# Attention with keys on partitions, exp without a maximum, sums from a column of ones, and the old program kept in a branch

## The chip, the cores and the metric

One NeuronCore of one Trainium2 chip runs the whole program. The metric is the device time of one execution in microseconds (us), lower is better. Everything is float32 unless a line says otherwise.

## The reference

Inputs: q, k, v of 4 batch entries x 8 heads x 768 tokens x 64, eight memory keys and values for each head, a router `w_gate` (512 x 8), and two weight matrices for each of eight experts. Cut to what matters:

```python
for c in range(S // 32):                       # chunks of 32 queries
    k_ctx = k[:, :, max(0, 32*c - 16) : min(S, 32*c + 32 + 8)]
    k_full = concat([mem_k, k_ctx]); v_full = concat([mem_v, v_ctx])
    scores = q_c @ k_full.T / 8
    a = exp(scores - max(scores)); a = a / (sum(a) + 1e-9)
    out[:, :, c] = a @ v_full
x = out as (3072 tokens, 512)
logits = x @ w_gate; e = argmax(logits); gate = softmax(logits)[e]
y = gate * (relu(x @ w1[e]) @ w2[e])
```

## The kernel before

The program has three stages that follow one another.

**Attention** (lines 155 to 235). A block is 96 queries (three chunks) of one batch entry with all 8 heads; there are 32 blocks, 8 for a batch entry. The 8 memory keys and the 120 keys that the three chunks can see are 128 keys. `load` (five transfers on SP's queue, 704 KB for a block) brings k, memory k, q, v and memory v, three blocks ahead. `turn_qk` transposes q and k on PE into the PSUM tiles `tq` and `tk`; ACT scales q out of PSUM (L170), DVE copies k (L174). `scores` puts **queries on partitions**: a bfloat16 matmul writes the additive mask (L182), eight head matmuls add q times k (L185, 128 columns each), DVE takes the negated maximum of each row (L187), ACT does one exp for each head with that maximum as bias and sums the row in the same instruction (L191; the sum shows as a second record, ACTIVATION_READ_ACCUMULATOR). The values need the keys on partitions, so `turn_ex` transposes each head's exponentials on PE (`te`, L199) and DVE or ACT copies them out (L201). `values` multiplies (L209), DVE divides by the sums (L212, L213, L215) and POOL's queue writes the block x to memory (L218). `turn_xb` transposes x for the router (L224, L226), `logits` multiplies by `w_gate` (L235) into one PSUM tile per batch entry, and `route` runs after each eighth block.

The order of the work around the change is set in two places: the loop after `route` runs the steps of different blocks interleaved (scores of block i, values of i-2, logits of i-3), and the compiler's scheduler then orders each engine's instructions; an engine runs them in that order. PSUM tiles come from rotating pools: `ps_t` (three buffers) serves `tq`, `tk`, `te` and `tx`; a buffer is written again only after its reader has emptied it.

**Slots** (L313 to L351). Counts of tokens per expert, then 32 small matmuls (`who`, L343) find which token stands in which row of which slot of 128 tokens.

**Experts** (L358 to L407). 31 slots, each with 2 MB of w1 and 2 MB of w2 fetched on SP's queue (L360, L362), a gather of 128 rows of x (L364), four transposes, 32 matmuls of the first layer (L387, 128 columns), 8 of the second (L404, 512 columns), and a scatter of the result (L407).

The profile shows each float32 matmul as two PE instructions (a transpose as one), each with its own weight load (PEld).

Of the kernel before, what the change touches and what calls it, by code (L numbers as in the profile page):

```python
# [10 lines left out]
F32 = mybir.dt.float32  # L11
BF16 = mybir.dt.bfloat16
I32 = mybir.dt.int32
AX_X = mybir.AxisListType.X
OP = mybir.AluOpType
AF = mybir.ActivationFunctionType
PSUM = bass.MemoryType.PSUM
DRAM = bass.MemoryType.DRAM

B, H, S, D = 4, 8, 768, 64  # attention  # L20
NMEM = 8
CHUNK, LEFT, RIGHT = 32, 16, 8
QB = 96  # queries of a block: three chunks
NQB = S // QB  # blocks of a batch entry
NB = B * NQB  # blocks in all
BAND = QB + LEFT + RIGHT  # keys that a block's chunks see; with the memory 128
N, DM, E, F = B * S, H * D, 8, 1024  # experts
NS = N // 128 + E - 1  # slots of 128 tokens of one expert: enough for any routing
FAR = 4096.0  # a row index past the end
NEG = -1e30  # L30
# [5 lines left out]

def _consts():
    p = np.arange(128)
    c = {}
# [5 lines left out]
    c["token"] = p[:, None] + QB * np.arange(NB)[None]  # L45
    # additive mask of a block = chunk_of.T @ mask_*: row g holds chunk g's keys
    c["chunk_of"] = p[:, None] == np.arange(QB)[None] // CHUNK
    for name, qb in (("mask_first", 0), ("mask_mid", 1), ("mask_last", NQB - 1)):
        m = np.zeros((128, 128))
        key = p[NMEM:] - NMEM + band_start(qb)  # L50
        for g in range(QB // CHUNK):
            q0 = QB * qb + CHUNK * g
            seen = (key >= max(0, q0 - LEFT)) & (key < min(S, q0 + CHUNK + RIGHT))
            m[g, NMEM:] = np.where(seen, 0.0, NEG)
        c[name] = m
    at, k = {}, 0
# [3 lines left out]
    pack = np.concatenate([np.asarray(v).astype(np.float32) for v in c.values()], axis=1)  # L60
    return np.ascontiguousarray(pack), at


@with_exitstack
def kernel(
    ctx: ExitStack,
# [11 lines left out]
    nc = tc.nc  # L78
    mm, turn = nc.tensor.matmul, nc.tensor.transpose
# [6 lines left out]

    cpool = ctx.enter_context(tc.tile_pool(name="cpool", bufs=1))
    lpool = ctx.enter_context(tc.tile_pool(name="lpool", bufs=4))
    apool = ctx.enter_context(tc.tile_pool(name="apool", bufs=2))
    rpool = ctx.enter_context(tc.tile_pool(name="rpool", bufs=2))  # L90
    wpool = ctx.enter_context(tc.tile_pool(name="wpool", bufs=2))
    mpool = ctx.enter_context(tc.tile_pool(name="mpool", bufs=2))
    dpool = ctx.enter_context(tc.tile_pool(name="dpool", bufs=1, space=DRAM))
    ps_s = ctx.enter_context(tc.tile_pool(name="ps_s", bufs=2, space=PSUM))
    ps_t = ctx.enter_context(tc.tile_pool(name="ps_t", bufs=3, space=PSUM))
    ps_o = ctx.enter_context(tc.tile_pool(name="ps_o", bufs=2, space=PSUM))
    ps_r = ctx.enter_context(tc.tile_pool(name="ps_r", bufs=1, space=PSUM))

    x_dram = dpool.tile([N, DM], F32, name="x_dram")

# [1 line left out]
    pack, at = _consts()  # L102
    cst = cpool.tile([128, pack.shape[1]], F32, name="cst")
    nc.scalar.dma_start(cst, nc.inline_tensor(pack, name="c_pack").ap())

    def const(name):
# [3 lines left out]
    ident, tri, iota, slot0, rev, token = (  # L110
        const(n) for n in ("ident", "tri", "iota", "slot", "rev", "token")
    )
# [8 lines left out]
    ones = cpool.tile([128, 128], F32, name="ones")  # L121
# [3 lines left out]

    # q turned: of each pair of heads two copies, the other head's rows zero
    qTs = [cpool.tile([128, H // 2, 2, QB], F32, name=f"qT{i}") for i in range(2)]
    for i, t in enumerate(qTs):
        (nc.vector, nc.gpsimd)[i].memset(t, 0.0)

    # routing of all tokens: token 96 t + p at [p, t]
    onehot = cpool.tile([QB, NB, E], F32, name="onehot")
# [5 lines left out]

# [1 line left out]
    st = [dict() for _ in range(NB)]  # L140
# [87 lines left out]
    lg = {}  # L228
# [9 lines left out]

# [1 line left out]
    def small(shape, name, dt=F32):  # L240
        return rpool.tile(shape, dt, name=name)

    def route(b):
# [6 lines left out]
        nc.vector.reduce_max(top, l, axis=AX_X)  # L250
        # the first of the largest
        eq = small([QB, NQB, E], "eq")
# [4 lines left out]
        nc.vector.tensor_tensor(oh, bc(rev[0:QB], 1, NQB), bc(first, 2, E), op=OP.is_equal)  # L257
        # its probability: exp(0) over the sum
        nc.vector.tensor_tensor(l, l, bc(top, 2, E), op=OP.subtract)
# [4 lines left out]
        nc.vector.reciprocal(gate[:, sl], total)  # L264
        # the token's rank among its expert's tokens
        for t in range(t0, t0 + NQB):
# [43 lines left out]

# [1 line left out]
    cnt = ps_r.tile([128, E], F32, tag="r", name="cnt")  # L312
# [17 lines left out]

    # who is in slot a, row b: sums with one term over the tokens
    own = cpool.tile([QB, NB, E], F32, name="own_all")
# [19 lines left out]

# [1 line left out]
    ms = [dict() for _ in range(NS)]  # L354
# [71 lines left out]


# [1 line left out]
_INS = ["q", "k", "v", "mem_k", "mem_v", "moe_w_gate", "moe_w1", "moe_w2"]  # L429
# [24 lines left out]
```

## Time and profile before

| | |
|---|---|
| median of 3 runs | 760.68 us (759.02 to 760.82) |
| profiled execution | span 758.7 us, first to last instruction; no separate time is listed for it |
| attention, up to the last logits | 0 to 264 us |
| slots, up to the first gathered rows | 264 to 298 us |
| experts | 298 to 749 us |
| busy over the span | PE 690.3 us (91%), PEld 547.1 (72%), DVE 195.9 (26%), ACT 184.1 (24%), POOL 88.7 (12%) |
| moved by DMA | 175.06 MB, mean 231 GB/s |

How to read it: the shares over the whole span mix three stages, so the table by stage and the order of time inside one block say more than the totals. The span and the timed median differ by 2.0 us; the sum below is made against the span and then carried to the median.

### The profile page before, as it was taken

What the parts mean: (1) busy time and instruction counts of PE and PEld (TensorE: products, weight loads), DVE (VectorE), ACT (ScalarE), POOL (GpSimd) and SP (SyncE); (2) the same over time, 40 slices, a digit from 0 to 9 for tenths busy, and PEclk for the clock granted to TensorE, in tenths of its full rate; (3) what the DMA queues carried; (4) which work ended last, traced back from release to release, by engine and by line L of the source; (5) the groups of instructions that cost most, each with busy time, mean ns of one, the idle gap of its engine ahead of it and who ended that gap; (6) DMA issues with size and microseconds to landing.
All of it is one profiled execution on the core that took longest, in us unless ns stands there. A gap on an engine that the chain in (4) does not pass through costs nothing. (4 is left out here: it accounts for less than half of the span.)

```text
span 758.7 us, 11768 instructions
## 1 busy us (share of the span) xinstructions
PE 690.3 (91%) x4670; PEld 547.1 (72%) x4670; DVE 195.9 (26%) x438; ACT 184.1 (24%) x675; POOL 88.7 (12%) x133
## 2 busy tenths in 40 slices
PE   5889898888888746999999999999999999999994
PEld 4788787778778646767766776776776776776672
DVE  2555655665655531010010010010010001001000
ACT  3556556465645400001001000100100100100100
POOL 0000100100010122011111111111111111111010
PEclk9999899999989955999999999999999999999998
DMA  9545454455540148699989899899899899899830
GB/s 213 133 121 130 98 124 123 107 134 120 125 99 22 43 176 332 219 331 319 332 313 328 313 333 340 303 330 345 307 334 331 307 339 323 308 326 335 302 111 0
DMA packets 148438, 175.06 MB, mean 231 GB/s; under 512 B 95582, under 2 KB 95582, under 8 KB 148384
## 3 DMA queue, kind: packets, MB, share of 16 engines
q1 hardware_dynamic: 140704, 153.10, 62.4%
q0 software_dynamic: 7008, 20.72, 7.5%
q8 instruction: 37, 0.61, 0.3%
q10 hardware_dynamic: 672, 0.50, 0.2%
q14 instruction: 17, 0.14, 0.1%
HBM read 161.71 MB, written 14.42 MB: 232 GB/s over the span
## 5 line engine op out<-in xcount | busy, mean ns | idle before, releaser
L387 PEld LDWEIGHTS ph<-xsT,w 128*128 128x128 f32 x1984 | 227.2, 193 | 14.7 <-issue 14.4
L387 PE MATMUL ph<-xsT,w 128*128 128x128 f32 x1984 | 227.5, 276 | 0.0
L404 PE MATMUL py<-w,h 128*128 128x512 f32 x496 | 218.0, 592 | 0.0
L404 PEld LDWEIGHTS py<-w,h 128*128 128x128 f32 x496 | 91.8, 190 | 103.8 <-issue 103.8
L396 DVE TENSOR_SCALAR h<-ph 128x512 f32<-128x512 f32 x31 | 21.5, 692 | 402.5 <-issue 381.7
L191 ACT ACTIVATE ex<-sc,top 96x128 f32<-96x128 f32 x256 | 89.8, 357 | 65.7 <-DVE top L187 64.1
L406 ACT ACTIVATE y<-py,gates 128x512 f32<-128x512 f32 x31 | 21.3, 688 | 317.9 <-PE py L404 317.9
L185 PE MATMUL sc<-kT,qT 128*96 128x128 f32 x512 | 72.8, 290 | 1.1 <-DVE kT L174 1.1
L185 PEld LDWEIGHTS sc<-kT,qT 128*96 128x96 f32 x512 | 63.3, 176 | 1.8 <-ACT qT L170 1.2
L407 POOL DMA_INDIRECT out_dram<-y,dst x31 | 31.5, 1017 | 241.2 <-ACT y L406 241.2
L209 PE MATMUL o<-vn,eT 128*96 128x64 f32 x512 | 56.5, 245 | 1.6 <-DVE eT L201 1.3
L209 PEld LDWEIGHTS o<-vn,eT 128*96 128x96 f32 x512 | 52.8, 166 | 3.2 <-DVE eT L201 2.6
L187 DVE TENSOR_REDUCE top<-sc 96x4 f32<-96x512 f32 x64 | 44.0, 687 | 24.0 <-PE sc L185 24.0
L364 POOL DMA_INDIRECT xs<-x_dram,src x31 | 30.3, 977 | 169.5 <-PE txs L375 148.3
L191 ACT ACTIVATION_READ_ACCUMULATOR ex<-sc,top 96x1 f32 x256 | 50.0, 195 | 0.0
L398 ACT ACTIVATE h<-ph 128x512 f32<-128x512 f32 x31 | 18.5, 598 | 125.4 <-PE ph L387 125.4
L199 PE MATMUL te<-cst,ex 96*128 96x96 f32 x256 | 35.8, 269 | 9.8 <-ACT qT L170 9.8
L218 POOL DMA_DIRECT2D x_dram<-x x32 | 16.7, 522 | 228.8 <-DVE x L215 228.8
L170 ACT ACTIVATE qT<-tq 64x384 f32<-64x384 f32 x64 | 31.1, 486 | 40.7 <-PE tq L167 39.9
L199 PEld LDWEIGHTS te<-cst,ex 96*128 96x128 f32 x256 | 27.9, 153 | 14.8 <-ACT qT L170 14.7
L182 PE MATMUL sc<-cst 128*96 128x512 bf16 x64 | 24.9, 392 | 14.2 <-ACT ex L191 9.1
L235 PEld LDWEIGHTS lg_ps<-wg,xT 128*96 128x96 f32 x256 | 24.1, 164 | 13.0 <-DVE xT L226 12.5
(74 smaller groups left out, 372.5 us busy)
## 6 DMA issues: line engine op xcount, KB each, us to landing
w<-in_moe_w_dram SPq DMA_DIRECT2D x62, 2048.0 KB
kn<-in_k_dram SPq DMA_DIRECT2D x32, 240.0 KB
vn<-in_v_dram SPq DMA_DIRECT2D x32, 240.0 KB
qn<-in_q_dram SPq DMA_DIRECT2D x32, 192.0 KB
x_dram<-x POOLq DMA_DIRECT2D x32, 192.0 KB, 2.6
kn<-in_mem_k_dram SPq DMA_DIRECT2D x32, 16.0 KB
vn<-in_mem_v_dram SPq DMA_DIRECT2D x32, 16.0 KB
xs<-x_dram,src POOLq DMA_INDIRECT x31, 7.0
```

Source lines behind the costliest of these rows:

```text
L170: nc.scalar.activation(s["qT"][sl, :, x], tq[sl], AF.Copy, scale=D**-0.5)
L182: mm(sc, lhsT=const16("chunk_of"), rhs=bc(mask, 1, 4), start=True, stop=False)
L185: mm(sc[:, j], lhsT=s["qT"][:, h // 2, h % 2], rhs=s["kT"][:, h // 2], start=False, stop=j == 3)
L187: nc.vector.tensor_reduce(top, sc, axis=AX_X, op=OP.max, negate=True)
L191: nc.scalar.activation(ex[:, j], sc[:, j], AF.Exp, bias=top[:, j : j + 1], accum_out=s["sum"][:, h : h + 1])
L199: turn(te[:, j], s["ex", g][:, j], ident[0:QB, 0:QB])
L209: mm(s["o"][:, h], lhsT=s["eT", g][:, j], rhs=s["v"][:, h], start=True, stop=True)
L235: mm(lg["ps"][:, t], lhsT=s["xT"][:, c], rhs=wg[:, c], start=c == 0, stop=c == DM // 128 - 1)
L364: nc.gpsimd.indirect_dma_start(out=s["x"], out_offset=None, in_=x_dram, in_offset=bass.IndirectOffsetOnAxis(ap=src[:, a : a + 1], axis=0),)
L387: mm(ph[:, f], lhsT=s["w1"][:, c, c0 : c0 + 128], rhs=s["xT"][:, c], start=c == 0, stop=c == DM // 128 - 1,)
L404: mm(py, lhsT=s["h"][:, f], rhs=s["w2"][:, f], start=f == 0, stop=f == F // 128 - 1)
L407: nc.gpsimd.indirect_dma_start(out=out, out_offset=bass.IndirectOffsetOnAxis(ap=dst[:, a : a + 1], axis=0), in_=y, in_offset=None, bounds_ ...
```

## The change

The old program is kept whole, under the name `general`, with its pools renamed. A new program, `ordinary`, runs first; `general` stands in a branch behind it that is taken when a check of the sums fails. In `ordinary` the slots and experts are the old text; the attention is new:

- **q and k are turned a half batch entry (384 tokens) at a time**, with three sets of four 128 x 128 transposes for q and three for k. They are loaded with 3 transfers of 256 KB each (row j holds tokens 3p + j), so the copies out of PSUM write every third column of kT and qT. The memory keys are turned once and POOL copies them into kT after every 48 keys of a block, so that a window of 128 columns of kT is the block's memory and keys.
- **Scores have keys on partitions**: one matmul for a pair of heads with 192 columns, no mask matmul; the mask is the bias of the exp (0 or -1e30 for each key), one exp for each chunk of 32 queries over all heads; no maximum is subtracted.
- **Values** take the exponentials as they stand (no `te`, no copies); v has a 65th column of ones, so column 64 of the result is the sum. The 1e-9 is left out.
- Reciprocals of all sums are kept; at the end every one is compared with 1.0 and 1e-30, and `good` says whether all are inside.
- v is loaded with three transfers for a block (parts of its keys, memory, the other keys); `ps_t` has two buffers and now also serves the logits and the ranks; the score tile takes two banks.

```diff
+    def load_half(m):
+        b, hf = divmod(m, 2)
+        for name, src in (("q", q), ("k", k)):
+            t = half[m][name] = lpool.tile([128, NT, H, D], F32, name=f"{name}n")
+            by = src[b, :, HALF * hf : HALF * hf + HALF].rearrange("h (p t) d -> p t h d", t=NT)
+            for j in range(NT):
+                nc.sync.dma_start(t[:, j], by[:, j])
...
+    def turn_half(m, j):
...
+        tk = ps_t.tile([128, H // 2, 128], F32, tag="t", name="tk")
+        for a in range(H // 2):
+            turn(tk[:, a], half[m]["k"][:, j, 2 * a : 2 * a + 2].rearrange("p h d -> p (h d)"), ident)
+        by = tk.rearrange("p a (n f c) -> p a n f c", n=NQB // 2, f=2)
+        for f in range(2):
+            c0 = (QB // 2 + NMEM) * f + j
+            nc.vector.tensor_copy(
+                kT[:, :, hf * NQB // 2 : (hf + 1) * NQB // 2, c0 : c0 + QB // 2 - NT + 1 : NT], by[:, :, :, f]
+            )
...
+        for x in range(2):
+            sl = slice(D * x, D * x + D)
+            nc.scalar.copy(qT[sl, :, x, j : j + HALF - NT + 1 : NT], tq[sl])
...
+    def scores(i):
...
+        sc = ps_s.tile([128, 2, 512], F32, tag="s", name="sc")
+        for a in range(H // 2):
+            o = sc[:, a // 2, 2 * QB * (a % 2) : 2 * QB * (a % 2) + 2 * QB]
+            mm(
+                o.rearrange("p (x t) -> p x t", x=2),
+                lhsT=kT[:, a, w0 : w0 + WIN],
+                rhs=qT[:, a, :, q0 : q0 + QB],
+                start=True,
+                stop=True,
+            )
...
+        for g in range(3):
+            sl = slice(CHUNK * g, CHUNK * g + CHUNK)
+            nc.scalar.activation(
+                ex4[:, :, :, sl], sc4[:, :, :, sl], AF.Exp, bias=mask[:, 3 * x + g : 3 * x + g + 1], scale=D**-0.5
+            )
...
+    def values(i):
...
+        for g in range(2):
+            o = ps_o.tile([QB, 4, D + 1], F32, tag="o", name="o")
+            for j in range(4):
+                h = 4 * g + j
+                mm(o[:, j], lhsT=s["ex"][:, h], rhs=s["v"][:, h], start=True, stop=True)
+            inv = inv_all[:, i, 4 * g : 4 * g + 4]
+            nc.vector.reciprocal(inv, o[:, :, D])
+            nc.vector.tensor_tensor(s["x"][:, 4 * g : 4 * g + 4], o[:, :, 0:D], bc(inv, 2, D), op=OP.mult)
...
+    for i in range(NB + 3):
+        m = i // (NQB // 2)
+        if i % (NQB // 2) == 1 and m + 2 < 2 * B:
+            load_half(m + 2)
+        if i + 2 < NB:
+            load_v(i + 2)
+        if i < NB:
+            scores(i)
+        if i % (NQB // 2) < NT and m + 1 < 2 * B:
+            turn_half(m + 1, i % (NQB // 2))
+        if 0 <= i - 3 < NB:
+            logits(i - 3)
+        if 0 <= i - 1 < NB:
+            values(i - 1)
+        if 0 <= i - 2 < NB:
+            turn_xb(i - 2)
...
+    nc.vector.tensor_scalar(good, okp[0:1], float(QB * 2 * NB * H), None, op0=OP.is_equal)
...
+    ordinary(tc, *args, good)
+    rv = nc.values_load(good[0:1, 0:1], min_val=0, max_val=1)
+    with tc.If(rv == 0):
+        general(tc, *args)
```

How the order of instructions moves, at three places. First PE in the middle of attention. Before, one block (names: `tq`, `tk` q and k turned, `te` exponentials turned, `sc` scores, `o` values, `tx` x turned, `lg_ps` logits; a row counts matmuls, and `x4` is four of them):

```order
L167 MATMUL tq<-cst,qn 128x96 x4
L173 MATMUL tk<-cst,kn 128x128 x4
L199 MATMUL te<-cst,ex 128x96 x8
L185 MATMUL sc<-kT,qT_97 96x128 x4
L209 MATMUL o<-vn,eT 96x64 x4
L185 MATMUL sc<-kT,qT_97 96x128 x4
L209 MATMUL o<-vn,eT 96x64 x2
L224 MATMUL tx<-cst,x 128x96 x4
L209 MATMUL o<-vn,eT 96x64 x2
L182 LDWEIGHTS cst_90
L182 MATMUL sc<-cst_90 96x512
L235 MATMUL lg_ps<-wg,xT 96x8 x4
```

Each block has all of it, and the scores of one block fill the time in which the values' exponentials are copied. Now, from one block's values to the next block's, with two of a half's three sets of turns between:

```order
L640 MATMUL o<-v_108,ex 96x65 x8
L594 MATMUL tk<-cst,kn 128x128 x4
L603 MATMUL tq<-cst,qn 128x128 x4
L664 MATMUL lg_ps<-wg,xT 96x8 x4
L616 MATMUL sc<-qT_100,kT 128x192
L652 MATMUL tx<-cst,x 128x96 x4
L616 MATMUL sc<-qT_100,kT 128x192 x2
L594 MATMUL tk<-cst,kn 128x128 x4
L603 MATMUL tq<-cst,qn 128x128 x4
L664 MATMUL lg_ps<-wg,xT 96x8 x4
L616 MATMUL sc<-qT_100,kT 128x192 x3
L640 MATMUL o<-v_109,ex 96x65 x8
```

The transposes of exponentials and the mask matmuls are gone, the scores are four matmuls instead of eight, and `tk`, `tq`, `lg_ps`, `tx` follow one another through the same two buffers of `ps_t`.

Second, SP's queue where attention ends (`good` is the check, `expi` the experts of the slots, `w_2140` the first weights):

```order
L572 DMA v_107<-in_v_dram 48x8x64
L883 TENSOR_LOAD good
L883 ISA x2
L806 TENSOR_LOAD expi
L806 ISA x2
L808 ISA
L808 DMA w_2140<-in_moe_w_dram 128x4x1024
```

The load of `good` into SP's register stands ahead of the first load of `expi`, and so ahead of the weights. Third, the end of POOL's queue before `general` begins:

```order
L855 DMA out_dram<-y,dst 3072x512 x5
L883 TENSOR_LOAD good
L884 COMPARE_AND_BRANCH
L189 MEMSET qT_4461 128x768
L194 MEMSET seen 96x8
```

The load and the branch come behind the last scatter; PE, ACT and DVE have the same two behind their last instruction.

## Rows read from the trace of the kernel before

**Rows 1.** The page, busy tenths of PE and granted PE clock in 40 slices

```profile
PE   5889898888888746999999999999999999999994
PEclk9999899999989955999999999999999999999998
```

**Rows 2.** Busy time by stage: us, then PE, PEld, DVE, ACT, POOL, clock, DMA share, GB/s

```profile
0.00:9.00 9.00, 2.81 (x10) 1.59 (x10) 1.94 (x4) 2.25 (x3) 0.99 (x6) 1.00 0.85 198
9.00:264.00 255.00, 221.41 (x1984) 199.49 (x1985) 144.57 (x331) 141.76 (x609) 21.46 (x56) 0.97 0.46 111
264.00:298.00 34.00, 15.98 (x74) 15.24 (x73) 9.25 (x42) 0.26 (x1) 7.44 (x12) 0.50 0.67 265
298.00:749.00 451.00, 450.09 (x2604) 330.74 (x2604) 40.15 (x62) 39.84 (x62) 57.85 (x58) 1.00 0.86 301
```

**Rows 3.** Timeline of POOL, two blocks: start, us, what

```profile
120.54 0.51 POOL L218 DMA_DIRECT2D x_dram<-x  x1 [6.68 <-DVE x L215]
127.74 0.51 POOL L218 DMA_DIRECT2D x_dram<-x  x1 [6.69 <-DVE x L215]
```

**Rows 4.** Timeline of PE's weight loads in one block

```profile
121.72 0.76 PEld L235 LDWEIGHTS lg_ps<-wg,xT 128*96 128x96 f32 x8 [0.43 <-DVE xT L226]
...
123.26 0.45 PEld L173 LDWEIGHTS tk<-cst,kn 128*128 128x128 f32 x4
123.67 0.42 PEld L199 LDWEIGHTS te<-cst,ex 96*128 96x128 f32 x4
...
125.80 0.78 PEld L209 LDWEIGHTS o<-vn,eT 128*96 128x96 f32 x8
126.50 0.90 PEld L185 LDWEIGHTS sc<-kT,qT 128*96 128x96 f32 x8
...
127.69 0.40 PEld L224 LDWEIGHTS tx<-cst,x 96*128 96x128 f32 x4
128.03 0.42 PEld L209 LDWEIGHTS o<-vn,eT 128*96 128x96 f32 x4
```

**Rows 5.** The same of the experts: end of a second layer, then a first layer

```profile
502.32 0.19 PEld L387 LDWEIGHTS ph<-xsT,w 128*128 128x128 f32 x1 [0.24 <-issue]
502.75 7.11 PEld L387 LDWEIGHTS ph<-xsT,w 128*128 128x128 f32 x63 [0.24 <-issue]
```

**Rows 6.** Groups of instructions: busy us, mean ns of one, idle before

```profile
L191 ACT ACTIVATE ex<-sc,top 96x128 f32<-96x128 f32 x256 | 89.8, 357 | 65.7 <-DVE top L187 64.1
...
L174 DVE COPY kT<-tk 128x512 f32<-128x512 f32 x32 | 22.1, 692 | 29.8 <-PE tk L173 29.8
...
L398 ACT ACTIVATE h<-ph 128x512 f32<-128x512 f32 x31 | 18.5, 598 | 125.4 <-PE ph L387 125.4
...
L226 DVE COPY xT<-tx 128x384 f32<-128x384 f32 x32 | 17.8, 557 | 1.3 <-PE tx L224 1.3
...
L213 DVE RECIPROCAL inv<-inv 96x8 f32<-96x8 f32 x32 | 6.3, 198 | 1.0
```

**Rows 7.** Timeline, DVE's start after the scores of rows 4

```profile
126.11 0.69 DVE L187 TENSOR_REDUCE top<-sc 96x4 f32<-96x512 f32 x1 [0.32 <-PE sc L185]
```

**Rows 8.** Timeline of the start, the first scores

```profile
9.17 3.70 PE L185 MATMUL sc<-kT,qT 128*96 128x128 f32 x16 [0.88 <-DVE kT L174]
```

**Rows 9.** Timeline of PE, DVE and SP around the slots

```profile
263.47 0.84 PE L235 MATMUL lg_ps<-wg,xT 128*96 128x8 f32 x8 [0.65 <-DVE xT L226]
...
273.18 0.16 DVE L329 TENSOR_SCALAR expi<-expf 1x31 int32<-1x31 f32 x1
...
274.33 0.43 SPq L360 DMA_DIRECT2D w<-in_moe_w_dram  x1
...
298.04 1.97 PE L375 MATMUL txs<-cst,xs 128*128 128x128 f32 x8 [6.37 <-DMA xs<-x_dram,src]
```

**Rows 10.** The last scatter in the timeline, and the page's median to landing

```profile
749.17 0.99 POOL L407 DMA_INDIRECT out_dram<-y,dst  x1 [13.03 <-ACT y L406]
...
out_dram<-y,dst POOLq DMA_INDIRECT x31, 7.1
```

More of the change, by code (lines that the diff above doesn't have):

```diff
@@ L34, in band_start, with _consts_general @@
     return min(max(QB * qb - LEFT, 0), S - BAND)
-def _consts():
+def _consts_general():
     p = np.arange(128)
@@ L61, in _consts, with window, column, runs_of @@
     return np.ascontiguousarray(pack), at
+HALF = S // 2
+NT = HALF // 128
+WIN = 128
+PER = QB + NMEM
+KW = NQB * PER
+NV = 6
+def window(qb):
+    return min(max(PER * qb - LEFT, 0), KW - WIN)
+def column(c):
+    blk, r = divmod(c, PER)
+    if QB // 2 <= r < QB // 2 + NMEM:
+        return "mem", r - QB // 2
+    return "key", QB * blk + (r if r < QB // 2 else r - NMEM)
+def runs_of(qb):
+    out = []
+    for p in range(WIN):
+        kind, x = column(window(qb) + p)
+        if out and out[-1][1] == kind and out[-1][2] + out[-1][3] == x:
+            out[-1][3] += 1
+        else:
+            out.append([p, kind, x, 1])
+    return out
+def _consts():
+    p = np.arange(128)
+    c = {}
+    c["ident"] = np.eye(128)
+    c["tri"] = np.triu(np.ones((128, 128)), 1)
+    c["iota"] = np.broadcast_to(p, (128, 128))
+    c["slot"] = np.broadcast_to(128 * np.arange(NS), (128, NS))
+    c["rev"] = np.broadcast_to(E - np.arange(E), (128, E))
+    c["token"] = p[:, None] + QB * np.arange(NB)[None]
+    m = np.zeros((128, 3, 3))
+    for x, qb in enumerate((0, 1, NQB - 1)):
+        for g in range(3):
+            q0 = QB * qb + CHUNK * g
+            for i in range(WIN):
+                kind, t = column(window(qb) + i)
+                if kind == "key" and not max(0, q0 - LEFT) <= t < min(S, q0 + CHUNK + RIGHT):
+                    m[i, x, g] = NEG
+    c["mask"] = m.reshape(128, 9)
+    at, k = {}, 0
+    for name, v in c.items():
+        at[name] = (k, v.shape[1])
+        k += v.shape[1]
+    pack = np.concatenate([np.asarray(v).astype(np.float32) for v in c.values()], axis=1)
+    return np.ascontiguousarray(pack), at
 @with_exitstack
-def kernel(
+def general(
     ctx: ExitStack,
@@ L85, in bc @@
         return ap[idx].to_broadcast(shape)
[L87 to L102, printed above, removed]
+    cpool = ctx.enter_context(tc.tile_pool(name="g_cpool", bufs=1))
+    lpool = ctx.enter_context(tc.tile_pool(name="g_lpool", bufs=4))
+    apool = ctx.enter_context(tc.tile_pool(name="g_apool", bufs=2))
+    rpool = ctx.enter_context(tc.tile_pool(name="g_rpool", bufs=2))
+    wpool = ctx.enter_context(tc.tile_pool(name="g_wpool", bufs=2))
+    mpool = ctx.enter_context(tc.tile_pool(name="g_mpool", bufs=2))
+    dpool = ctx.enter_context(tc.tile_pool(name="g_dpool", bufs=1, space=DRAM))
+    ps_s = ctx.enter_context(tc.tile_pool(name="g_ps_s", bufs=2, space=PSUM))
+    ps_t = ctx.enter_context(tc.tile_pool(name="g_ps_t", bufs=3, space=PSUM))
+    ps_o = ctx.enter_context(tc.tile_pool(name="g_ps_o", bufs=2, space=PSUM))
+    ps_r = ctx.enter_context(tc.tile_pool(name="g_ps_r", bufs=1, space=PSUM))
+    x_dram = dpool.tile([N, DM], F32, name="g_x_dram")
+    pack, at = _consts_general()
     cst = cpool.tile([128, pack.shape[1]], F32, name="cst")
-    nc.scalar.dma_start(cst, nc.inline_tensor(pack, name="c_pack").ap())
+    nc.scalar.dma_start(cst, nc.inline_tensor(pack, name="g_pack").ap())
     def const(name):
@@ L429, with kernel @@
+@with_exitstack
+def kernel(ctx, tc, *args):
+    nc = tc.nc
+    gpool = ctx.enter_context(tc.tile_pool(name="gpool", bufs=1))
+    good = gpool.tile([1, 1], I32, name="good")
+    ordinary(tc, *args, good)
+    rv = nc.values_load(good[0:1, 0:1], min_val=0, max_val=1)
+    with tc.If(rv == 0):
+        general(tc, *args)
 _INS = ["q", "k", "v", "mem_k", "mem_v", "moe_w_gate", "moe_w1", "moe_w2"]
```

275 lines of the change are left out of this document (added).

## Prediction

> **What bounds the kernel now.** I read the 40 slices first [rows 1]: PE's digits are 8 and 9 in the first third and 9 to the end, with a hole of two slices between, where the clock digit is 5. So there are three stages and PE sets the pace in two of them. The busy time by stage [rows 2] puts numbers on this. In the experts (298 to 749 us) PE is busy 450.09 of 451 us at clock 1.00; their text does not change. In the slots (264 to 298) the engines wait for one another at half clock; that chain does not change either. In attention (9 to 264) PE is busy 221.41 of 255 us, DVE 144.57, ACT 141.76, and DMA has a share of 0.46. The change can win only there, and only what it takes from PE's queue or from PE's waits. The writes of x give attention's pace: 120.54 and 127.74, so 7.20 us for a block [rows 3].
>
> **PE's prices.** I take the step between the starts of weight loads inside a block [rows 4], as PE works in order and these show when it goes on. Of values' 16 instructions, 8 go from 125.80 to 126.50: 0.70 us, so 1.40 for a block. Four transposes of k take 123.26 to 123.67, 0.41. Four of x take 127.69 to 128.03, 0.34. Logits take 0.76. Scores now have 192 columns, a width no row shows. Below it lies 128 columns: 63 loads in 7.11 us, 0.113 each; above it 512 columns: 502.32 to 502.75, 0.43 each [rows 5]. Between them in proportion it is 0.113 + 0.317 x 64/384 = 0.166 us, so 1.33 us for a block's eight instructions.
>
> **PE's work after.** A block costs 1.40 (values; one column more changes nothing I can see, since logits with 8 columns take about as long per instruction, 0.095, as values with 64, 0.088) + 1.33 (scores) + 0.34 + 0.76 = 3.83 us. A set of turns (k and q) costs 0.82, and there are three sets in four blocks, so six in eight: 4.9. Routing adds some 0.6 in eight blocks. Eight blocks are 30.6 + 4.9 + 0.6 = 36.1 us, 4.5 a block. What goes is the mask matmuls, the eight `te` and half the score instructions.
>
> **PE's waits after.** I walked the new order on PE over eight blocks, with these steps. An engine starts 0.31 us after PE goes on to the next group (125.80 to 126.11 [rows 4, 7]). DVE's copies cost 557 ns for 384 elements and 692 for 512 [rows 6], so 1.05 ns an element and 153 fixed: 0.42 for 256. ACT takes 598 ns for 512 [rows 6]. Three kinds of wait remain.
> - In a set of turns the logits need the buffer of `tk`, which two kT copies must empty: 0.31 + 2 x 0.42 + 0.05 = 1.2 us, of which `tq` covers 0.41. Some 0.75 each, six times: 4.5 us.
> - Where x is turned straight after its values, the second half of x comes 0.31 + 0.20 (reciprocal [rows 6]) + 0.42 + 0.05 = 0.98 us after them, less 0.2 for turning the first half: 0.8, in four blocks of eight: 3.2 us.
> - Routing's ranks wait for POOL: some 0.6 us.
>
> So eight blocks take 36.1 + 8.3 = 44.4 us, 5.55 a block. PE would be busy 81% of that against 87% now, so I keep the clock near its 0.97.
>
> **What lies beside it.** ACT: three exps of 256 elements, 357 ns for 128 [rows 6] plus 107, so 0.46 each, 1.4; two q copies of 0.60 in each set, three sets in four blocks, 0.9; half a copy of x, 0.25: 2.6 us of 5.55. DVE: two reciprocals and two products 1.24, kT copies 0.63, half of xT 0.28, logits 0.2, routing and rows 0.6: 3 us. DMA: 640 KB to load where it was 704, the same 192 to write; 0.46 x 7.2 = 3.3 us of full share becomes 3.1. Were these covers gone, each would be paid at its own figure, and PE's is the longest. SP issues 4.5 transfers for a block where it issued 5, and each load of q and k waits only for a buffer that was turned a half earlier.
>
> **Start, end, and the sum.** The first scores stood at 9.17 [rows 8]. Now all six loads of the first half must land, with the constants and memory 1.89 MB; at the 198 GB/s of the first 9 us [rows 2] that is 9.5 us, some 10 with the issue. Then the last turns (0.82), their copies (1.5): 12.3, plus scores 1.33 and their exps 1.55: the first values at 15.2. 28 blocks at 5.55 are 155.4. The last four turn nothing: 3 x 4.1 = 12.3 to the last values, then 1.40 + 0.98 + 0.20 + 0.84 + 0.76 = 4.2 to the end of the last logits: 187.1, where it was 264.3 (263.47 + 0.84 [rows 9]). That is **77 us less**.
> The check of the sums (three DVE instructions, 1.4 us) stands between the last x and the last logits' copy, when DVE has nothing else: 0; without that cover 1.4. SP's load of `good` stands ahead of the weights. After `expi` is written (273.34) it took 1.0 us to the first fetch [rows 9]; such a load more, even if all of it came late, lies under the 23.7 us from that fetch to the first gathered rows at 298.04. At the end each engine loads `good` and branches; POOL does so after its last scatter's issue (749.17 + 0.99), and landing takes 7.1 us [rows 10], which covers a load of 1.0 and as much again and more. No row shows the branch: bounds are 0 (all under the landing) and 5 us (nothing under it but two microseconds); I take 1, near the covered end. Span 758.7 - 77.2 + 1 = 682.5; the median stands 2.0 above the span, so **685 us**.
> [...]
>
> **The rivals.**
> - *Waits hidden better.* If PE's waits shrink to a third, 5.55 becomes 4.9: 19 us less, 660 to 676. For it: the scheduler interleaved; against it: both buffers of `ps_t` are in every wait above. 0.15.
> - *The turned copies are slow.* The rows give DVE's and ACT's copies for unbroken runs only [rows 6]; kT and qT are written at every third column. If the part by element doubles, a kT pair takes 0.53 us longer and a q pair 0.85; 21 sets in the flow and the start pay 0.5 to 0.9 each, 11 to 19 us: 698 to 706; with threefold 720. No gain at all would be left only from 77/21 = 3.7 us a set. 0.22. [...]
> - *DMA bounds.* Three strided loads at half the rate would make 6.2 us a block and 705 to 725; against it: pieces are 256 bytes, as before. 0.03.
> - *The old program runs too.* A single reciprocal above 1 or under 1e-30 makes `good` 0; then `general` follows with its 759: **1,440 us**, slower. The sums have some 56 to 64 terms of exp of small scores (inputs are 0.1 times a normal), so reciprocals near 0.02: far inside. 0.03, with every other way to be slower.
>
> **How the numbers follow.** My forecast, 676 to 698, has 0.56; hidden waits 0.15, slow copies 0.22, DMA 0.03, slower 0.03, no change 0.01. The range leaves out the ends of both neighbours: from 662 (waits nearly gone: 77 + 23 less) to 718 (copies almost threefold). About 0.3% (2 us) is what a measurement of this kernel can tell from no change. Faster 0.96, same 0.01, slower 0.03.
>
> **What would show it.** Right: writes of x 5.5 us apart; last logits near 187; eight score instructions a block at 0.166; PE waiting for `tk` buffers and x; `who` and the experts as long as before; the last scatter's landing still last. Wrong: kT copies over 0.55 us or q copies over 0.8 (second rival); PE waiting for `kn`, `qn` or v (third); first values well after 15; the clock digit falling in attention; an end more than 10 us after the last scatter's issue.

## The result and the profile after

The change took **721.33 us** (median of four runs, 720.99 to 725.84) where the kernel before took 760.75: a ratio of 0.9497, 95% interval 0.9464 to 0.9530. Here and below, medians are over all executions, while ratios leave out one execution each of e2 (729.81), e8 (705.64) and e12 (705.79), which lay over 1.5% above the fastest of their program, at its lowest mean clock. The forecast was 685 us with a range of 662 to 718. The sign was right, and half of the forecast saving came: 39.4 us of 75.7. The profiled execution has a span of 719.6 us where the sum had 682.5, so 37.1 us are to be found.

The page of after, as [rows 1] of before:

```profile
PE   2888898898883699999999999999999999999991
...
PEclk9999969969955579999999999999999999999996
```

Attention is shorter, but the clock digit now falls to 6 inside it twice and is 5 at its end. The table by stage answers to [rows 2], with the stages cut at the first values, the end of the last logits and the first gathered rows:

```profile
0.00:21.54 21.54, 7.20 (x38) 5.66 (x38) 5.41 (x9) 7.73 (x11) 3.96 (x15) 1.00 1.12 188
21.54:219.24 197.70, 173.93 (x1322) 157.31 (x1322) 82.89 (x292) 79.19 (x154) 22.15 (x58) 0.87 0.59 120
219.24:252.88 33.64, 15.76 (x73) 15.37 (x72) 9.21 (x43) 0.26 (x1) 7.27 (x12) 0.50 0.70 265
252.88:705.25 452.37, 451.29 (x2604) 331.97 (x2604) 40.14 (x62) 39.80 (x62) 57.72 (x58) 0.99 0.84 301
```

| stage | forecast | after | difference |
|---|---|---|---|
| to the first values | 15.2 | 21.54 | +6.3 |
| first values to the last logits | 171.9 | 197.70 | +25.8 |
| slots, as before | 33.7 | 33.64 | -0.1 |
| experts, as before | 451.1 | 452.37 | +1.2 |
| last scatter to the end (9.5 before, + 1) | 10.5 | 14.35 | +3.8 |

So the overrun lies in attention, in its start, and at the end. In attention the clock is 0.87, where before had 0.97. The stretches of half clock, found from windows of half a microsecond and so known to about a microsecond, are these four:

```profile
51.00:54.50 3.50, 3.50 (x21) 3.41 (x20) 1.20 (x4) 1.20 (x3) 0.51 (x1) 0.52 0.05 10
92.00:105.50 13.50, 13.02 (x71) 12.06 (x70) 3.80 (x13) 6.20 (x11) 1.02 (x2) 0.50 0.21 48
143.00:157.00 14.00, 13.38 (x73) 12.59 (x73) 4.58 (x15) 6.21 (x11) 1.02 (x2) 0.51 0.18 41
197.50:219.24 21.74, 17.80 (x99) 15.26 (x97) 7.07 (x23) 2.16 (x5) 2.05 (x4) 0.51 0.13 37
```

They are 52.7 us long, and TensorE is busy for 47.7 us of them. What that costs is read from the same work at both levels, the 16 weight loads of a block's values, in the timeline of PEld:

```profile
134.96 1.52 PEld L640 LDWEIGHTS o<-v,ex 128*96 128x96 f32 x16
...
145.35 2.68 PEld L640 LDWEIGHTS o<-v,ex 128*96 128x96 f32 x16
```

2.68 / 1.52 is 1.76, so 47.7 us of work would have been 27.1: by this estimate **20.6 us went to the clock**. What came before a fall is seen in windows of 2 us:

```profile
83.00:85.00 2.00, 1.85 (x20) 1.71 (x18) 1.68 (x8) 0.11 (x1) 0.00 (x0) 1.00 1.14 271
85.00:87.00 2.00, 0.85 (x5) 0.85 (x6) 0.49 (x2) 1.09 (x3) 0.51 (x1) 1.00 1.24 227
87.00:89.00 2.00, 1.59 (x13) 1.33 (x11) 0.74 (x2) 0.38 (x1) 0.40 (x1) 1.00 1.11 235
89.00:91.00 2.00, 1.50 (x15) 1.44 (x16) 0.36 (x3) 1.28 (x2) 0.00 (x0) 1.00 0.70 129
91.00:93.00 2.00, 1.71 (x11) 1.15 (x10) 1.22 (x3) 0.67 (x1) 0.00 (x0) 0.73 0.01 1
```

TensorE waited for several things one after another, here 2.4 of the 8 us from 85 on, and then the clock fell. In before the same is seen: 8 us of its even flow, and the 8 us ahead of its fall at 148:

```profile
124.00:132.00 8.00, 6.92 (x68) 6.11 (x67) 4.83 (x9) 5.19 (x22) 0.51 (x1) 1.00 0.47 115
140.00:148.00 8.00, 5.02 (x48) 4.17 (x47) 4.70 (x17) 3.25 (x17) 2.10 (x9) 1.00 0.44 108
```

TensorE idles 1.1 us of the first and 3.0 of the second. No single gap of PE in after between 22 and 197 us is longer than 1.3 us. As far as these rows show, a fall goes with waits that are bunched, and not with the stage's share of busy time: in after's attention PE is busy 173.9 of 197.7 us, 88% (some 87% if the clock's 20.6 us are taken from both), and before's stood at 87% with a clock of 0.97. Why the waits of after bring more half clock than those of before (52.7 us to 18.0) is not shown beyond this.

The waits themselves (PEld's, first values to last logits) stand where the prediction had them, the buffers behind `tq` first, then x, at 7.3 and 6.9 us where its sum has 15.8 and 11.2 for 28 blocks; the wait for exponentials is new:

```profile
PEld lg_ps L664 <- PE tq L603: 7.3, 9, 0.9
PEld tx L652 <- DVE x L644: 6.9, 19, 0.7
PEld sc L616 <- ACT ex L629: 6.1, 10, 1.4
```

The turned copies, for the second rival:

```profile
L606 ACT COPY qT<-tq 64x512 f32<-64x512 f32 x48 | 40.0, 834 | 31.8 <-PE tq L603 29.8 <-DVE kT L598 1.6
...
L598 DVE COPY kT<-tk 128x256 f32<-128x256 f32 x48 | 20.5, 487 | 26.6 <-PE tk L594 23.9 <-POOL kT L586 2.7
```

### The profile page after: what moved, and what is told of

It is laid out like the page before. It is cut to its first block, busy times and chain, and to the rows that moved or that the text cites. A ratio compares the mean times of both kernels' runs of the same rounds, so it can differ in the third digit from the quotient of the medians.

```text
span 719.6 us, 9964 instructions
## 1 busy us (share of the span) xinstructions
PE 648.2 (90%) x4036; PEld 510.3 (71%) x4036; DVE 137.6 (19%) x406; ACT 127.0 (18%) x228; POOL 92.1 (13%) x144
## 5 line engine op out<-in xcount | busy, mean ns | idle before, releaser
L844 DVE TENSOR_SCALAR h<-ph 128x512 f32<-128x512 f32 x31 | 21.5, 692 | 403.7 <-issue 381.7
L616 PE MATMUL sc<-qT,kT 128*128 128x192 f32 x256 | 58.3, 354 | 9.2 <-ACT ex L629 4.2
L640 PE MATMUL o<-v,ex 128*96 128x65 f32 x512 | 58.5, 276 | 1.4 <-ACT ex L629 1.4
L640 PEld LDWEIGHTS o<-v,ex 128*96 128x96 f32 x512 | 57.0, 193 | 1.9 <-ACT ex L629 1.9
L616 PEld LDWEIGHTS sc<-qT,kT 128*128 128x128 f32 x256 | 42.3, 199 | 13.0 <-ACT ex L629 6.1
L629 ACT ACTIVATE ex<-sc,cst 128x256 f32<-128x256 f32 x96 | 38.5, 471 | 70.8 <-PE o L640 63.2
L606 ACT COPY qT<-tq 64x512 f32<-64x512 f32 x48 | 40.0, 834 | 31.8 <-PE tq L603 29.8
L664 PE MATMUL lg_ps<-wg,xT 128*96 128x8 f32 x256 | 30.5, 246 | 8.8 <-DVE kT L598 5.2
L652 PE MATMUL tx<-cst,x 96*128 96x96 f32 x128 | 24.2, 287 | 4.9 <-DVE x L644 2.8
L644 DVE TENSOR_TENSOR x<-o,inv_all 96x256 f32<-96x256 f32 x64 | 26.9, 420 | 2.1
L823 PE MATMUL txs<-cst,xs 128*128 128x128 f32 x124 | 19.4, 283 | 6.9 <-DMA xs<-x_dram,src 6.9
L598 DVE COPY kT<-tk 128x256 f32<-128x256 f32 x48 | 20.5, 487 | 26.6 <-PE tk L594 23.9
```

The costliest lines, as they stand in the source:

```text
L606: nc.scalar.copy(qT[sl, :, x, j : j + HALF - NT + 1 : NT], tq[sl])
L616: mm(o.rearrange("p (x t) -> p x t", x=2), lhsT=kT[:, a, w0 : w0 + WIN], rhs=qT[:, a, :, q0 : q0 + QB], start=True, stop=True,)
L629: nc.scalar.activation(ex4[:, :, :, sl], sc4[:, :, :, sl], AF.Exp, bias=mask[:, 3 * x + g : 3 * x + g + 1], scale=D**-0.5)
L640: mm(o[:, j], lhsT=s["ex"][:, h], rhs=s["v"][:, h], start=True, stop=True)
L644: nc.vector.tensor_tensor(s["x"][:, 4 * g : 4 * g + 4], o[:, :, 0:D], bc(inv, 2, D), op=OP.mult)
L652: turn(tx[:, c], s["x"][:, 128 * c : 128 * c + 128], ident[0:QB, 0:QB])
```

## The experiments

All run the whole program; the diffs are against the change unless another is named. The table has the medians and ratios to before, and of the profiled execution the first values, the time from there to the last logits, the half clock in that time, TensorE's idle time in it (its length less PE's busy time), and the slots. One execution of each is profiled.

| run | us | ratio, 95% | first values | to last logits | half clock | PE idle | slots |
|---|---|---|---|---|---|---|---|
| before | 760.75 | 1 | 21.7 | 242.6 | 18.0 | 31.4 | 33.7 |
| after | 721.33 | 0.9497 (0.9464-0.9530) | 21.5 | 197.7 | 52.7 | 23.8 | 33.7 |
| e1 fill | 737.32 | 0.9711 (0.9681-0.9740) | 23.9 | 208.2 | 34.5 | 19.8 | 33.7 |
| e2 contiguous | 717.69 | 0.9411 (0.9377-0.9445) | 19.0 | 198.7 | 57.2 | 23.2 | 33.6 |
| e3 memory first | 721.63 | 0.9500 (0.9471-0.9529) | 23.6 | 195.0 | 46.0 | 23.5 | 33.7 |
| e4 no branch | 722.06 | 0.9487 (0.9436-0.9537) | 24.2 | 204.1 | 63.7 | 22.9 | 33.7 |
| e5 e2 + buffers | 698.65 | 0.9165 (0.9142-0.9188) | 18.2 | 179.3 | 26.5 | 20.4 | 33.6 |
| e6 slots | 717.76 | 0.9418 (0.9402-0.9434) | 24.2 | 197.9 | 53.6 | 23.9 | 28.0 |
| e7 dense | 727.05 | 0.9570 (0.9522-0.9618) | 21.7 | 200.9 | 38.6 | 23.4 | 33.7 |
| e8 buffers | 696.95 | 0.9147 (0.9094-0.9200) | 19.9 | 175.0 | 24.8 | 15.3 | 33.7 |
| e9 e5 + fillers | 693.93 | 0.9119 (0.9085-0.9153) | 19.1 | 177.0 | 14.0 | 15.6 | 28.4 |
| e10 split only | 713.74 | 0.9403 (0.9368-0.9439) | 20.8 | 187.6 | 30.9 | 22.0 | 33.7 |
| e11 e8 + slots | 692.20 | 0.9103 (0.9077-0.9129) | 19.6 | 174.1 | 21.6 | 15.2 | 28.0 |
| e12 e11 + tail | 684.63 | 0.9005 (0.8977-0.9032) | 19.6 | 167.1 | 0 | 10.9 | 28.0 |

**e1: work where TensorE waits.** Three fillers in each set of turns, one in the turning of x, four more in the last blocks:

```diff
+    def filler(n):
+        for _ in range(n if "o" in spare else 0):
+            mm(spare["o"], lhsT=ident[:, 0:QB], rhs=ident, start=True, stop=True)
...
+        filler(3)
...
+            if c == 2:
+                filler(1)
...
+        if i >= NB - 4:
+            filler(4)
```

> Adds 111 filler matmuls of 128 columns (constants into columns of the value tiles that nothing reads, about 0.22 us each, 25 us of TensorE work): three in each set of turns, one while a block's x is turned, four more in each of the last four blocks. Theory A (the loss is clock: 52 us of attention at 0.50, where 16 weight loads of values take 2.68 us and not 1.52, some 22 us lost): the half-clock stretches of attention go or shrink to under 20 us, and the time falls although work is added, to 700 to 712 us. Rival (the half clock costs little, the loss is waits and copies): the fillers lie partly on the path, 722 to 745 us.

Between. Half clock fell from 52.7 us to 34.5; before the last blocks only 7 us are left of 31.0. But the time rose by 16 us. The logits still waited 6.8 us behind `tq`, and the fillers, which write columns of the value tiles, waited themselves until x had been read out of those tiles:

```profile
PEld o L578 <- DVE x L653: 9.7, 19, 0.9
```

So much of the added work ran behind a wait and not in it. The clock can be held, and this way costs more than it gives. The last four blocks stayed at 0.50 in spite of five fillers each.

**e2: unbroken copies.**

```diff
-            by = src[b, :, HALF * hf : HALF * hf + HALF].rearrange("h (p t) d -> p t h d", t=NT)
...
+                nc.sync.dma_start(t[:, j], src[b, :, r : r + 128].rearrange("h p d -> p h d"))
...
-            nc.scalar.copy(qT[sl, :, x, j : j + HALF - NT + 1 : NT], tq[sl])
+            nc.scalar.copy(qT[sl, :, x, 128 * j : 128 * j + 128], tq[sl])
```

> Loads q and k so that each turned tile holds 128 tokens in a row; the copies into qT and kT then write unbroken runs (kT in 7 pieces a half and not 6). Theory B (the writes at every third column are slow): a qT copy falls from 834 ns to about 600 and the time falls by 5 to 15 us, to 706 to 716. Theory A (clock): whatever the copies do, attention keeps its half-clock stretches and the time stays within 4 us of 721.

```profile
L605 ACT COPY qT<-tq 64x512 f32<-64x512 f32 x48 | 27.8, 579 | 34.4 <-PE tq L602 34.1
```

The copies are what theory B says, 579 ns for 834. The time does not decide between the theories: it is 3.6 us less by the medians, inside theory A's 4 us, and some 6.5 less by the ratios (0.9411 for 0.9497 of 761), near the top of theory B's range. The profiled execution speaks for theory A: the start gave 2.5 us, and from the first values on it is 198.7 us with 57.2 us of half clock. The earlier start is not the copies' alone, since with tokens in a row the first scores need no third set of turns; they come at 14.24 us instead of 18.71, ahead of it:

```profile
14.24 0.76 PE L615 MATMUL sc<-qT,kT 128*128 128x192 f32 x2
14.84 0.60 PE L594 MATMUL tk<-cst,kn 128*128 128x128 f32 x4
```

**e3: memory keys first.** On SP's queue this stands ahead of q and k:

```diff
-        nc.scalar.dma_start(mk[NMEM * b : NMEM * b + NMEM], mem_k[b].rearrange("h m d -> m h d"))
+        nc.sync.dma_start(mk[NMEM * b : NMEM * b + NMEM], mem_k[b].rearrange("h m d -> m h d"))
```

> The four loads of memory keys go first on SP's queue instead of last on ACT's. TensorE turned nothing before 9.56 us, since the memory keys' turns stand first in its order and their load landed then. If that is what made the start late, the first half is turned as its loads land, the first scores come at 13 to 15 us instead of 18.7, and the time falls by 4 to 5.5 us (715.5 to 717.5). If the chain of qT copies sets the start, the first scores come at 16 to 18 and the time falls by 1 to 2 us.

Neither; the first scores came later, at 19.36, and the time is the same. Its timeline of PE:

```profile
4.90 0.60 PE L577 MATMUL tm<-cst,mk 32*128 32x32 f32 x4 [4.90 <-DMA mk<-in_mem_k_dram]
9.80 1.11 PE L594 MATMUL tk<-cst,kn 128*128 128x128 f32 x4 [4.29 <-DMA kn<-in_k_dram]
...
13.56 1.12 PE L603 MATMUL tq<-cst,qn 128*128 128x128 f32 x4 [0.57 <-ACT qT L606]
...
16.44 1.12 PE L603 MATMUL tq<-cst,qn 128*128 128x128 f32 x4 [0.91 <-ACT qT L606]
```

The memory keys are turned 4.7 us earlier, to no use: k's first transposes wait for `kn` until 9.80. The start is bound by that load, and behind it by three sets of turns that pass through two PSUM buffers, each held by q copies of 1.7 us a pair.

**e4: no branch.**

```diff
-    rv = nc.values_load(good[0:1, 0:1], min_val=0, max_val=1)
-    with tc.If(rv == 0):
-        general(tc, *args)
```

> The load of good, the branch and the old program behind it are left out (the sums are still checked, nothing reads the result). After's span ends 14.35 us after its last scatter's issue, before's 9.5. If the branch adds the difference: end 9.5, time less by 4 to 5.5 us (716 to 717.5). If the end has another cause: within 1 us of 721.

```profile
714.29 0.98 POOL L855 DMA_INDIRECT out_dram<-y,dst  x1 [13.03 <-ACT y L854]
```

The span ends at 723.8, so 9.51 us behind the last scatter's issue, as before and not 14.35: the load of `good` and the branch together are the end's 4.84 us. Yet the median did not fall: in the profiled execution attention had 11 us more of half clock, and the first values came 2.6 us later. The four executions of this one program bear on the price: two with a mean clock of 0.935 took 718.75 and 718.87 us, two with 0.923 took 725.25 and 725.61. A mean of 0.012 less over 722 us is 17.3 us more at half clock; 6.6 / 17.3 is 0.38 us for each, and 52.7 x 0.38 = 20 us, close to the estimate above. By the same sum executions of e8 (693.38 us at 0.950, 698.71 at 0.940), e10 (709.23 at 0.944, 718.61 at 0.926) and e12 (683.16 at 0.980, 687.45 at 0.972) give 0.37 to 0.39. This price is an estimate: how the starts of the executions without a profile differed is not on record, and the clock is not all that varies, as after's own four lie 4.9 us apart at 0.927 to 0.932.

**e5: shorter waits, the same work.** On e2:

```diff
-    ps_s = actx.enter_context(tc.tile_pool(name="ps_s", bufs=2, space=PSUM))
-    ps_t = actx.enter_context(tc.tile_pool(name="ps_t", bufs=2, space=PSUM))
+    ps_s = actx.enter_context(tc.tile_pool(name="ps_s", bufs=3, space=PSUM))
+    ps_t = actx.enter_context(tc.tile_pool(name="ps_t", bufs=3, space=PSUM))
...
+        for g2 in range(2):
+            sc = ps_s.tile([128, 4, QB], F32, tag="s", name="sc")
...
+                    ex[:, 4 * g2 : 4 * g2 + 4, sl], sc[:, :, sl], AF.Exp, bias=mask[:, 3 * x + g : 3 * x + g + 1], scale=D**-0.5
```

> On the contiguous loads (e2): the score tile is split in two of one bank each (three buffers, six exps of 128 elements a block in place of three of 256), so the pool of turned tiles has three buffers. It takes away waits and leaves TensorE's work as it is. In after, TensorE's loads waited 7.3 us for the logits' buffer behind tq, 6.1 us for the scores' buffer behind ex and some 6 us for buffers of tq. If waits are the loss: 10 to 17 us under e2, 700 to 708 us. Theory A (clock): TensorE still has half-clock stretches of 40 us and more in attention, which give most of it back: 709 to 717 us.

The time goes past the first theory's, 19.0 us under e2, but not by its mechanism: TensorE's idle time fell by only 2.8 us (23.2 to 20.4), and the half clock by 30.7 (57.2 to 26.5), which at 0.38 is 11.7 us, and with TensorE busy all that time (0.76 / 1.76 of it) 13.3. Together that is 14.5 to 16 of the 19.4 us between first values and last logits. Here the shorter waits pay mostly through the clock. My bound of 40 us of half clock for theory A was wrong.

**e6: the slots' clock.** Four matmuls of 512 columns ahead of `who`, four of 464 behind it.

```diff
+    for _ in range(4):
+        mm(ft, lhsT=ident[0:QB], rhs=row_of[:, NB - 4 : NB], start=True, stop=True)
     who = ps_r.tile([128, 3, NS], F32, tag="r", name="who")
...
+    for _ in range(4):
+        mm(ft[0:NS, 0:464], lhsT=dstf, rhs=cst, start=True, stop=True)
```

> After, with four filler matmuls of 512 columns between the counts and who, where TensorE waits 8.4 us for the entries, and four of 464 columns behind who, where it waits 6.9 us for the gathered rows; their results are not read. In after all of the slots ran at 0.50 and who took 13.97 us. If the clock is what the slots' matmuls pay for: it rises before or in who, who takes 7 to 10 us, and the first layer starts at full clock: time less by 5 to 9 us (712 to 716). If the fillers do nothing for the clock: who 13.97 again and the time the same or up to 4 us more.

```profile
232.08 13.97 PE L791 MATMUL who<-ent,row_of 96*128 96x93 f32 x64 [8.40 <-POOL ent L787]
```

```profile
229.24 6.40 PE L791 MATMUL ft<-row_of,cst 96*128 96x512 f32 x8 [2.72 <-DVE row_of L712]
235.48 7.28 PE L794 MATMUL who<-ent,row_of 96*128 96x93 f32 x64
```

The first view is after's, the second e6's. `who` takes 7.28 us, where it took 13.97 in after; the slots take 28.0 instead of 33.7. The median is 3.6 us less, short of the 5 to 9 expected (some 6 by the ratios): in the profiled execution the first experts gave back 1.5 (453.9 for 452.4 us), and the start, which the edit does not touch, came 2.6 us later.

**e7: before's wide matmuls put back.**

```diff
+        for g in range(2):
+            mm(sc[:, g], lhsT=dense[:, 0:128], rhs=dense, start=True, stop=True)
```

> After, with two bfloat16 matmuls of 512 columns ahead of each block's scores, into the score tile, which the scores then overwrite: the place and width of before's mask matmuls, which the change took out. 64 of them at about 0.22 us are 14 us of work more. Theory A (the change took from TensorE the wide work that held its clock up): the half-clock stretches between 50 and 160 us go or shrink to under 12 us of the 30 there, and the time falls by 0 to 8 us (713 to 721) in spite of the work; TensorE's loads of values step at 1.52 us for 16 throughout 30 to 190 us. Rival (the clock does not depend on it): the half-clock time stays at 50 and the time rises by 8 to 15 us, to 729 to 736.

Not clear: half clock before the last blocks fell from 31.0 us to 14, not to 12, and the time rose by 5.7, between the two ranges (its executions lie 10 us apart, at mean clocks of 0.934 to 0.940). The trace has 46 of the 64 added matmuls, at some 0.38 us each, so its idle time is too long by the rest. That the clock paid for part of this work fits, but is not shown. What the mask matmuls did for before's clock stays open.

**e8 and e10: which half of e5.** e8 is e5's edit on after, with the copies at every third column; e10 takes from it:

```diff
-    ps_t = actx.enter_context(tc.tile_pool(name="ps_t", bufs=3, space=PSUM))
+    ps_t = actx.enter_context(tc.tile_pool(name="ps_t", bufs=2, space=PSUM))
```

> The split score tile and third buffer of e5 without e2's contiguous loads, so with the writes at every third column (qT copy 834 ns). If the split alone keeps the clock up between 20 and 170 us: half clock there under 8 us, and the time 699 to 707, e5's 698.7 plus up to the 3 us by which the start and the copies are slower. If the slow copies are what lets the clock fall: half clock there 20 us and more, and 710 to 719.

> The split score tile of e8 with three one-bank buffers and six exps a block, but only two buffers for turned tiles as in after (one bank of PSUM lies idle). It tells which half of e8 keeps the clock up. If the waits for tq's and the logits' buffers let it fall: half clock of 15 us and more between 20 and 170 us, 706 to 718. If the scores' waits for ex did: as e8, 694 to 701.

```profile
PEld lg_ps L662 <- PE tq L603: 7.3, 11, 0.9
```

e8 has no half clock between 20 and 170 us (1.00 throughout) and takes 696.95, under its range and as little as e5: the slow copies cost nothing that shows once there is a third buffer. e10, whose row stands above, keeps the logits' wait behind `tq`, falls to half clock twice in that time (10.5 us, where 15 and more was expected), idles 22.0 us, and takes 713.74. In e8 that wait is gone from the list. By the medians the split alone gives 7.6 us and the buffer 16.8 more. In the profiled executions the buffer gives 12.6 us of attention (187.6 to 175.0): TensorE idles 6.7 us less, and 6.1 us less of half clock are worth some 2.3 at 0.38, so the buffer pays in the main as a wait. The split's 10.1 us of attention (197.7 to 187.6) come with 21.8 us less of half clock, some 8.3 at 0.38, and 1.8 less of idle time. Here is e8's attention by stage, to be held against after's 173.93 of 197.70 at 0.87:

```profile
19.86:194.83 174.97, 159.69 (x1323) 145.86 (x1322) 83.13 (x292) 93.27 (x250) 22.16 (x58) 0.93 0.66 138
```

**e9: fillers in tail and slots.** e5 with e6's edit, and two fillers a block in the last six, in buffers of the scores.

> e5, with e6's fillers in the slots and, in the last six blocks, one filler of 256 columns and one of 512 beside the turns of x, where TensorE waits for x and for its copy; results not read. In e5 the clock is 0.50 from 174.5 us through the slots: a block takes 6.04 us there. Theory A: it stays at or near 1.00 in the tail, blocks of 4.2 to 5 us, slots of some 28 us: 685 to 693. If the fillers only add work: 699 to 706.

693.93, 0.9 us above theory A's range. The last blocks held 1.00 and came 4 to 5.3 us apart, but the fillers took the scores' buffers, the scores were put later, and the clock stood at 0.51 from 159 to 173 us, ahead of them.

**e11 and e12: what beats both kernels.** e11 is e8 with e6's edit. e12 adds to it:

```diff
+        if i >= NB - 5:
+            ft = ps_t.tile([128, 512], F32, tag="t", name="ft")
...
+            if i >= NB - 5 and c in (1, 3):
+                w = 64 * (c + 1)
+                mm(ft[:, 0 : 2 * w], lhsT=ident[0:QB], rhs=s["x"][:, 0 : 2 * w], start=True, stop=True)
```

> e8 with e6's fillers in the slots. e6 gained 5.7 us in the slots by its trace (33.7 to 28.0): 687 to 694 if that adds to e8's gain; 695 to 700 if the slots' gain is lost in the first experts, whose weights then land too late.

> e11 with one filler of 256 and one of 512 columns in each of the last five blocks, into a buffer of the turned tiles (so the scores' buffers stay free, unlike e9). In e8 the clock is 0.50 from 170 us on and the last four blocks take 6.04 us each. If the fillers keep it at 1.00: blocks of 4 to 4.8 us, 5 to 8 us under e11, 681 to 689. If the fall comes all the same: e11's time or up to 6 us more.

Both fell in the first of their cases: 692.20 and **684.63 us**, a ratio of 0.9005 to before. e12's table by stage and four writes of x in its last blocks (POOL):

```profile
19.62:186.68 167.06, 156.11 (x1342) 140.67 (x1342) 83.13 (x292) 93.44 (x250) 22.17 (x58) 1.00 0.70 145
186.68:214.63 27.95, 18.64 (x88) 11.97 (x89) 9.21 (x43) 0.26 (x1) 7.28 (x12) 0.80 0.64 241
```

```profile
172.96 0.51 POOL L644 DMA_DIRECT2D x_dram<-x  x1 [4.53 <-DVE x L642]
176.98 0.51 POOL L644 DMA_DIRECT2D x_dram<-x  x1 [3.51 <-DVE x L642]
181.00 0.51 POOL L644 DMA_DIRECT2D x_dram<-x  x1 [3.51 <-DVE x L642]
185.03 0.51 POOL L644 DMA_DIRECT2D x_dram<-x  x1 [3.51 <-DVE x L642]
```

The ten fillers are 8.4 us of TensorE's work more than e11 has, and the median is 7.6 us less, with 21.6 us of half clock gone: this is the plainest sign here that the half clock itself costs time. With the clock at 1.00 throughout, attention takes 167.1 us from its first values, where I had forecast 171.9; the last blocks, which in after were 6.0 us apart (204.73 to 210.76), are 4.0 apart, and I had 4.1. The fillers are in these numbers, and so is the third buffer, which the change did not have. That e12's time is near the 685 of the forecast is chance: it has a start 4.4 us later than forecast, the branch, the shorter waits of the third buffer, and slots 5.7 us shorter.

## Why the prediction was wrong

By its own steps:

- **"PE would be busy 81% of that against 87% now, so I keep the clock near its 0.97": the step that failed.** It took the clock from the stage's share of busy time. PE was in fact busy 88%, more than in before, and the clock was 0.87 all the same (1.00 in the windows between the four stretches, 0.50 to 0.52 in them): 52.7 us at half clock, which cost an estimated 20.6 of the 37.1 us. That half clock costs time is shown by e12 against e11 (more work, no half clock, less time) and borne out by e5 (idle time 2.8 us less, half clock 30.7 less, 19.4 us gained); the size rests on the steps of the weight loads at both levels and on the executions of e4, e8, e10 and e12. Held to the full clock, the forecast's pace was near:

```profile
53.88 0.51 POOL L646 DMA_DIRECT2D x_dram<-x  x1 [6.80 <-DVE x L644]
...
198.67 0.51 POOL L646 DMA_DIRECT2D x_dram<-x  x1 [3.47 <-DVE x L644]
```

  These are 24 blocks in 144.8 us. Two whole stretches of half clock lie in them, 26.4 us of busy time that cost 11.4; without these it is 5.56 us a block, against 5.55 forecast (the order is not quite the forecast's, as the next points say).
- **Start (+6.3).** The load term was right (forecast some 10, `kn` landed at 9.80 in e3). "Then the last turns (0.82), their copies (1.5)" was wrong: k's turns stand first in TensorE's order, so nothing of the half is turned before a load of k lands, and then three sets follow, not one. The end of it, in after (the set before the last, the last, the first scores):

```profile
13.85 0.66 PE L603 MATMUL tq<-cst,qn 128*128 128x128 f32 x4 [0.56 <-ACT qT L606]
14.34 0.60 PE L594 MATMUL tk<-cst,kn 128*128 128x128 f32 x4
16.26 0.66 PE L603 MATMUL tq<-cst,qn 128*128 128x128 f32 x4 [1.32 <-ACT qT L606]
18.71 1.86 PE L616 MATMUL sc<-qT,kT 128*128 128x192 f32 x10 [1.80 <-issue]
```

- **End (+3.8).** I took 1 us between bounds of 0 and 5; it was 4.84 (e4). The landing did not cover the load and the branch. No row stood behind the 5, so that the bound is so close is luck. No run here parts the load from the branch, or shows what either waits for.
- **PE's prices.** Right: by the starts of weight loads at clock 1.00, values took 1.41 us (59.25 to 60.66) against 1.40, eight score instructions 1.25 (86.14 to 87.39) against 1.33, logits 0.71 (71.70 to 72.41) against 0.76, a set's transposes of k 0.42 to 0.49 against 0.41. Of what lies beside PE, no row stood behind the 107 ns added for an exp of 256 elements; after's took 471 ns, 114 more than before's 357 for 128.

```profile
59.25 1.52 PEld L640 LDWEIGHTS o<-v,ex 128*96 128x96 f32 x16
60.66 0.45 PEld L594 LDWEIGHTS tk<-cst,kn 128*128 128x128 f32 x4
...
86.14 1.27 PEld L616 LDWEIGHTS sc<-qT,kT 128*128 128x128 f32 x8 [1.43 <-ACT ex L629]
87.39 0.30 PEld L594 LDWEIGHTS tk<-cst,kn 128*128 128x128 f32 x2
```

- **PE's waits.** The places were right (logits behind `tq`, x behind its values), and the scores' wait for `ex`, 6.1 us, was missing. All idle time was 23.8 us, against some 29 (8.3 for eight blocks). What was not seen is that these waits have a second price, the clock's (half clock of 52.7 us, and of 24.8 in e8). With 20.6 of attention's 25.8 us explained, some 5 remain. They stand in the first blocks: from the write of the first x (24.10) to that of the fifth (53.88) it is 29.8 us, where four blocks of the forecast are 22.2 and the half clock is worth some 1.3. By 53.88 TensorE had done the scores of nine blocks and nine sets of turns, where the sum has paid for five and six: work done early. No run tests whether that costs time in the end.
- **The rival of slow copies.** Its sign for q was met (834 ns, over 0.8), and for k not (487, under 0.55). Its price, 11 to 19 us, was not paid: e2, which also starts earlier, gained 3.6 us (6.5 by the ratios), and e8 loses nothing that shows by them. They run on ACT and DVE, which are busy 79.2 and 82.9 of attention's 197.7 us. Part by element, 579 to 834 ns over 512 elements is 0.50 ns more each. The rival's sum of 698 to 706 did not follow, as the copies were not what TensorE paid for.
- Slots and experts came as forecast; the check of the sums cost nothing that shows. DMA did not bound (its share of attention is 0.59), and `general` did not run. Of the signs named beforehand for being wrong, four came: q copies over 0.8 us, first values well after 15, the clock digit falling in attention, and an end more than 10 us after the last scatter's issue.

The range failed for the same reason: none of its ends had a row for the clock, though the slots stage [rows 2] stood at 0.50 in the trace of before, and the digits of [rows 1] showed that it falls inside attention too.

## What to carry to other kernels

A change that leaves TensorE as the pace can lose its clock though its share of busy time does not fall (88% here at a clock of 0.87, 87% before at 0.97); price the stage at both levels (here 1.76 times for the weight loads of a block's values), and put the half clock's price into the range wherever several waits follow one another in TensorE's order. Look for the buffer that strings these waits together before adding fillers: one more PSUM buffer gave 16.8 us by the medians, and fillers that waited for the same things as the work cost 16. Fillers paid in two places here, in the slots (e6) and in the last blocks (e12), where TensorE waits and nothing else is left for it to do.

## What the runs showed of the hardware

- In after, `who` ran for 14 us without a gap and the clock stayed at 0.50; in the first layer (from 254.78) it rose, to 0.96 in the window from 259 to 261:

```profile
232.00:240.00 8.00, 7.92 (x37) 7.92 (x38) 0.00 (x0) 0.00 (x0) 0.03 (x1) 0.50 1.00 381
240.00:246.00 6.00, 6.00 (x29) 5.81 (x28) 0.00 (x0) 0.00 (x0) 0.00 (x0) 0.50 1.04 414
...
257.00:259.00 2.00, 2.00 (x12) 2.00 (x10) 0.00 (x0) 0.00 (x0) 0.00 (x0) 0.50 0.47 133
259.00:261.00 2.00, 2.00 (x19) 2.00 (x19) 0.00 (x0) 0.21 (x1) 0.00 (x0) 0.96 0.01 2
```

- With the clock up beforehand (e6, 1.00 from 235.0 us on) the same `who`, from 235.48 us on, kept it and took 7.28 us.
- At the start of the program the recorded clock is 1.00 while the work steps at the lower rate: in e3 four turns took 1.06 to 1.12 us until 17.6 us, in after 0.60 to 0.66 from 13.85 on. With the slower steps (e1, e3, e4, e6) the first values came at 23.6 to 24.2 us, and at 21.5 in after.
- The same program falls to half clock for a different length of time from run to run, by some 17 us between executions of e4, worked out from their mean clocks. A difference of a few microseconds between two kernels with such falls says little without the clock beside it.
